# Q and K of pairs 6 to 15 turned in 32x32 blocks by VectorE and regrouped through DRAM, instead of turned by TensorE

## The chip, the core and the metric

One core of a Trainium2 chip runs the whole program. The metric is the device time of one execution in microseconds (us); the time of a kernel is the median of its runs. TensorE (PE) multiplies matrices and writes only to the eight PSUM banks, VectorE (DVE) and ScalarE (ACT) work on elements, GpSimd (POOL) and SyncE (SP) mostly issue transfers (DMAs) here. Each engine works through its own queue in order.

## The reference

Block-sparse attention with batch 4, 8 heads, 768 positions and head size 64, then an MLP mixer on the result:

```python
scores = scale * np.matmul(q, k.transpose(0, 1, 3, 2))
...
scores = np.where(mask, scores, -1000000000.0)
...
attn = attn / (np.sum(attn, axis=-1, keepdims=True) + 1e-09)
return np.matmul(attn, v).astype(np.float32)
...
h = np.maximum(xt @ w_tok1, 0.0) @ w_tok2
u = x + h.transpose(0, 2, 1)
h2 = np.maximum(u @ w_ch1, 0.0) @ w_ch2
return (u + h2).astype(np.float32)
```

The mask lets blocks of 32 positions see their neighbours, the first and the last block, and three drawn blocks each. The scores need Q and K with the head dimension on the partitions, while they are loaded with positions on the partitions, so both must be turned.

## The kernel before, in words

The 32 heads are worked as 16 **pairs** of two heads. For each pair the kernel loads K, Q and V as bf16 (`load_pair`, L458, issued by POOL; token 6p+c goes to partition p), and then:

- **Turn.** `relayout` (L786) copies the raw K or Q into a `lay` tile with the two heads side by side (L811, by VectorE or ScalarE, labels `l` and `L`). `transposes` (L853) turns it on TensorE against an identity matrix, six steps a tensor (label `t`): pairs 1 to 7 as full 128x128 tiles (L910), pairs 8 to 15 as two 64-row tiles at once (L875). A copy out of PSUM puts the result into `ktb` or `qtb`, one of four buffers each (L886 and L923, label `h`; L939 for pairs 1 to 3).
- **Scores.** `scores` (L962, matmul at L974, label `q`): 9 steps a pair, each four matmuls of 256 columns; from pair 4 on the two heads run in the two halves of the array. ScalarE takes the exponential (L984, `e`), VectorE multiplies by the mask (L1001, `x`, two operations for each third of a pair).
- **Values.** V is copied beside a column of ones (L808, `y` and `Y`), multiplied with the exponentials (L1113 with the whole array, L387 with half arrays, `v` and `V`), and VectorE divides (L1069 and L1126 with the line behind each, `n`, one for each third of a pair).
- **Mixer.** Per batch: token mixing (`f`, `g`, `k`, `K`; relus `af`, `ak`; adds `df`, `dk`), a turn of the sum (L1178, L1441, copies `w`), channel mixing (`c`, `C`; relus `r` at L1155 on ScalarE and L1157 on VectorE), and the stores (`o`, L1578 and L1633, issued by SP). The mixer of one batch runs between the attention of the next.

**The order of the work** is written out. `ORDER` (L38) holds a list of labels for each engine, and a planner (`Planner`, L127) walks through the lists with a cost in ns for each step and emits an instruction when its list and its inputs let it. The program that results is fixed: on the chip each engine does its list in that order and waits where an input is late. The costs place an instruction only among those of other engines' queues, such as which DMA issue or fence on SP comes first.

**Half-array chains.** `halves` (L377) sums in two rounds, with lower-case labels for the first and capitals for the second. The two row tiles swap banks in between, and the second round must not start before the first has ended. `fence` (L370, no-op at L373) sees to that: a no-op that waits for the last matmul of the first round, on SP, or on POOL once nearly all loads are through (`pool_free`). The second round's first matmuls wait for the no-op.

```python
late = pool_free.t is not None and pool_free.t < P.now
n = (nc.gpsimd if late else nc.sync).nop()
tc.add_manual_dep(n.ins, mm.ins.name, AFTER, reason=WHY)
```

**A path that is there but not taken.** For pairs from `NPE` on, `relayout` turns the raw tensor in blocks of 32x32 with two VectorE instructions (one a head, 128x384 elements each), and `through_dram` (L829) regroups the blocks: SP puts the tile out to DRAM (192 KB, label `b`) and gets it back in four transfers of 32 partitions (label `u`, runs of 192 elements). `scores` then reads keys with a step of six elements and queries in runs of 32 (L972, L973). Before, `NPE` is 16, so no pair takes it. The planner counts 1050 ns for the two block turns (`TURN`).

Of the kernel before, what the change touches and what calls it, by code (L numbers as in the profile page):

```python
# [28 lines left out]
def spell(text):  # L29

    steps = []
    for word in text.split():
        name = word.rstrip("0123456789")
        steps += [name] * int(word[len(name):] or 1)
    return steps
# [1 line left out]

ORDER = dict(  # L38
    pe=spell("""
        q s3 q s t6 q3 s q v t6 v2 q2 v2 t6 q t v t v t q t3 m q v2 q3 f v f5 v2 f2 q f3 v f q2 v2 q t4 f t  # L40
        f3 t2 f2 t2 v t2 q v f3 q v f3 t q v t4 q f t f2 t v q f9 q v f2 q f q f3 t v t3 v2 q t2 f7 q f3 q
        f2 v q v q v f t2 v f v t4 f q v f5 q t f t f3 t2 f q f v t2 f2 q v f t2 f q t v2 t q f t2 v2 t2 f q
        t f3 t2 f t g12 q f6 t3 g2 t2 g4 t g6 q2 f2 v t g2 t g2 f t2 g2 f3 q t v2 t q c3 q c q2 C4 c11 q C2
        q c C10 q v6 q c3 q c4 C q c C c C c2 C2 c q c3 C c C2 q C7 c C c2 q v9 c q2 C2 k6 C2 K c K c K q K
        c K c K q C4 k4 v4 k2 K4 v2 K2 v3 c v c v c v c3 V7 c2 V2 q V3 C5 q C3 c q c4 q c k c k2 c k2 t3 k
        t3 c2 q c2 k6 q C3 q C3 v9 t3 v t v t2 C2 v q C V12 q C3 q c4 q c3 t6 q c2 v12 q c2 v5 V v4 V v3 V4
        c V17 C V q C3 q C2 t C t5 q C3 t6 C2 q v24 V24 t6 c3 q c k5 q k c2 t K t4 K t K4 c q c2 v11 k v c2
        k2 t V t3 V2 t V t k V8 c K4 C2 k2 q C K2 C2 q C3 k5 t2 k t4 C2 k6 C2 v3 c v2 c v7 c2 t5 V4 t V2 C q
        C2 V C c4 q V5 C3 v C v11 q c2 V12 c6 q2 C8 c2 v12 c2 V4 q V8 C q C3 q c4 q C3 v3 C v9 c4 V q c2 V4
        c2 V2 q V5 C8 c v12 c q c V2 c V10 q C4 q c2 k5 c2 k t q C t C t4 C K C K5 q c8 v5 q v4 C6 v C2 v2  # L50
        k4 V12 q K4 k2 q K2 c3 q c q k6 c4 v9 t v3 t5 c V12 k2 c k4 c2 q v12 C q C V C V11 q C3 q v C4 v4 q
        C2 c2 v7 c2 t2 V9 t V3 t3 c q c3 q c v11 c q v c2 V4 v V4 v3 V C V v5 V2 v3 C2 q V C V4 q V C V2 C
        V4 C2 q C2 k C2 k2 v3 k3 q v5 K v K v2 K v K3 t3 V12 t3 c3 q c k4 q c K4 k2 c3 q K2 c2 q c2 k6 q C4
        q C2 t C t5 q C2 k2 C k4 q C2 v24 V14 q V7 c3 q c V3 q C4 c6 q c C c C t6 C2 c6 v C v2 C v8 C q C v
        c2 C6 V C v C V v2 V v4 V4 v3 V v V4 v13 V15 q V9 c2 q c2 k2 q k3 C2 q k C2 K v K v3 K3 v8 K q V12 q
        k4 c2 q c K3 c K k2 c4 K2 q C8 c4 q v7 C v k6 C v3 C v C k6 v12 V20 c2 q c2 V4 q C4 c2 q c9 q c C c
        v c v C2 v C4 q v4 c v c2 C v4 c2 V3 c V9 q C c C c2 q c6 C c v5 q v7 C6 V2 c v C V4 v V c C2 v V2 v
        C V v4 V v4 V C2 V C V11 C2 c4 k6 c k c k4 c k c6 k4 c k7 c4 k c4 C3 k4 C k5 C2 k3 c182
    """),
    act=spell("""  # L60
        p e37 h e ag e h e9 r e4 r e2 r e5 r l e4 w e3 h e10 h e2 h e l h e2 w e r e8 r e2 r e4 y ak e2 r e4
        h w e5 y e7 ak h e2 l e9 r e r e r2 e4 r e4 r e r e5 r e3 ak r2
    """),
    dve=spell("""
        Z3 z3 Y z H z H z H2 n S H2 Y n H2 m n2 af Y n df H L H n df H2 h L wf Y2 l2 n y af n h df2 n h n l
        wf l h af n l n x h df l df dg2 x wg wf n h x r x3 r n2 l x l x2 y x r x2 n3 l y x r y ak x dk2 n x
        r x h x w x3 n o l x h x2 y n l n x h2 o n2 x l2 x ak x2 l n dk2 l x h w o l h x2 n r n x r x n x r
        x l x n x n r x h r x l x n dk2 x w x n x2 y n x2 o l n h x2 n x n x o y n x2 dk2 x w y x h w o n x
        n x y h x4 n3 x3 ak n x dk2 x2 w2 x n2 r x2 n x3 o n2 dk3 w2 r9 o2 r2 o r4 o2 r o5
    """),  # L70
    sp=spell("""
        s2
    """),
)
AF = mybir.ActivationFunctionType
# [38 lines left out]
TURN = 1050.0  # L114
# [192 lines left out]
def kernel(  # L307
# [14 lines left out]
    B, H, S, D = q.shape  # L322
# [5 lines left out]
    NV = 4  # L328
    NR = 4
    NET = 4  # L330
    NPE = 16
    NT0 = 4

    sb1 = ctx.enter_context(tc.tile_pool(name="sb1", bufs=1))
# [451 lines left out]
    def relayout(p):  # L786
        lays = LAYS[p] = {}
        for nm in ("k", "q", "v") if p >= NT0 else ("v",):
            raw = raws.pop((nm, p))
            arr = arrive.pop((nm, p))  # L790

            def emit(eng, nm=nm, raw=raw):
                copy = nc.scalar.copy if eng == "act" else nc.vector.tensor_copy
                if nm != "v" and p >= NPE:
                    lay = sbw.tile([128, 2, 2, NC * 32], BF16, tag=f"{nm}lay", bufs=2, name=f"{nm}lay{p}")
                    for h in range(2):
                        to = lay[:, h, :, :]
                        if nm == "k":
                            to = to.rearrange("p g (j c) -> p g c j", c=NC)
                        else:  # L800
                            to = to.rearrange("p g (c j) -> p g c j", c=NC)
                        nc.vector.transpose(
                            out=to,
                            in_=raw[:, h, :, :].rearrange("p c (g e) -> p g c e", g=2),
                        )
                    lays[nm] = lay
                elif nm == "v":
                    copy(out=vaug[p % NV][:, :, :, 0:64], in_=raw)  # L808
                else:
                    lay = sbw.tile([128, NC, 2, D], BF16, tag=f"{nm}lay", bufs=2, name=f"{nm}lay{p}")  # L810
                    copy(  # L811
                        out=lay[:, :, :, :], in_=raw.rearrange("p h c d -> p c h d")
                    )
                    lays[nm] = lay

            deps = [arr]
            if nm == "v" and p >= NV:
                deps.append(pv_done[p - NV])
            if nm != "v" and p >= NT0 + 2:
                deps.append(qT_there[p - 2, 1])  # L820
            block = nm != "v" and p >= NPE
            lays[nm + "ev"] = P.op(("dve", "act") if p >= FORM["relay_act"] and not block else ("dve",),
                                  {"dve": TURN if block else 290.0, "act": 660.0}, deps, emit,
                                  label=("y" if nm == "v" else "l") if p >= FORM["relay_act"] else "Y" if nm == "v" else "L")
            copied[nm, p] = lays[nm + "ev"]
        va_there[p] = lays["vev"]
        return lays

    def through_dram(p):  # L829

        lays = LAYS[p]
        for nm, bufs, there in (("k", ktb, kT_there), ("q", qtb, qT_there)):
            where = stage[nm][p % 2]
# [128 lines left out]
    def scores(s, bank, done, rel, exps):  # L962
# [808 lines left out]
```

## Time and profile before

| | |
|---|---|
| median of 3 runs | 249.47 us (249.04 to 249.51) |
| the profiled execution, its own time | 249.75 us |
| its span, first to last instruction | 248.0 us |
| PE busy, share of the span | 241.2 us, 97% |
| VectorE busy | 187.6 us, 76% |
| ScalarE busy | 172.3 us, 69% |
| GpSimd busy | 49.6 us, 20% |
| granted TensorE clock | 0.997 |
| moved by DMA | 21.05 MB, 85 GB/s in the mean |

The profile is one execution. A row of a group reads: source line, engine, operation, output tile, inputs, shapes, count, then busy us and the mean ns of one, then the idle time of the engine just ahead of them and who ended it. PEld is TensorE's weight load, which runs beside the matmul ahead of it. A row of one line (the view by source line) gives shortest, median and longest ns and the first and last start. Rows with an engine name that ends in q (SPq, POOLq) are waits or DMA issues on that engine's queue. Matmuls overlap, so the time that one takes from PE is the distance to the next start and not its mean duration; the trace holds the starts.

Scores of pair 6 start at 64.9 us, those of pair 8 at 90.3, of pair 15 at 183.9; the last end at 198.2. The loads of all pairs are issued by 69.2 us.

### The profile page before, as it was taken

The page shows a single profiled execution, that of the slowest core. Times are in us where ns is not written, and L with a number is a line of the kernel's source. Part 1 is how long each engine was busy: PE and PEld are TensorE (multiplying, and loading weights), DVE is VectorE, ACT ScalarE, POOL GpSimd, SP SyncE. Part 2 cuts the span into 40 slices and gives each one's busy share as a digit, 9 for nine tenths or more (in the row PEclk, how much of TensorE's full clock was granted, in tenths as well). Part 3 has the DMA queues.
Part 4 walks back from the last instruction along what each step waited for, and adds up shares of the span by engine and source line. Part 5 has one row for each costly group of instructions (what it writes and reads, how often), then busy time and mean ns, then how long its engine had stood idle before and what let it go on. Part 6 is the DMA issues. An engine that isn't in the chain of part 4 may idle for free.

```text
span 248.0 us, 9867 instructions
## 1 busy us (share of the span) xinstructions
PE 241.2 (97%) x4446; PEld 175.2 (71%) x4450; DVE 187.6 (76%) x346; ACT 172.3 (69%) x188; POOL 49.6 (20%) x86
## 2 busy tenths in 40 slices
PE   7899989999999999999999999999999999999994
PEld 3689979876777667767778777777887656566442
DVE  5894977989879998999788887986788353388422
ACT  5999989998787988758989978988887610100000
POOL 8948987457510000000000000000000000000000
PEclk9999999999999999999999999999999999999998
DMA  7999999999980022020000022020000010004132
GB/s 172 161 206 207 211 204 203 205 201 201 201 134 3 4 87 90 3 87 3 3 3 3 4 90 83 7 89 3 3 3 5 3 76 11 0 3 157 57 127 85
DMA packets 18969, 21.05 MB, mean 85 GB/s; under 512 B 1328, under 2 KB 16320, under 8 KB 18928
## 3 DMA queue, kind: packets, MB, share of 16 engines
q0 software_dynamic: 15104, 12.98, 33.2%
q1 hardware_dynamic: 3280, 7.06, 7.5%
q8 instruction: 35, 0.57, 0.9%
q10 hardware_dynamic: 544, 0.39, 0.5%
q14 instruction: 6, 0.05, 0.1%
HBM read 26.74 MB, written 6.29 MB: 133 GB/s over the span
## 4 chain that ended last, share of the span: by engine, by line
PE 85%; DMA 5%; POOL 5%; DVE 3%; issue 1%; DVEq 0%; POOLq 0%
PE banks L387 50%; PE banks L974 12%; PE banks L1607 8%; PE banks L1542 6%; DMA kraw<-in_k_dram 5%; PE banks L1113 3%; POOL vraw L458 1%; PE banks L875 1%; PE banks L1382 1%; PE banks L910 1%; POOL kraw L458 1%; POOL qraw L458 1%; PE banks L1178 1%; DVE vaug L808 1%; PE banks L1362 1%
## 5 line engine op out<-in xcount | busy, mean ns | idle before, releaser
L984 ACT ACTIVATE et<-banks 128x1024 bf16<-128x1024 f32 x144 | 139.8, 1026 | 24.4 <-PE banks L974 22.8
L1001 DVE TENSOR_TENSOR et<-et,mask 128x992 bf16<-128x992 bf16 x72 | 65.2, 927 | 3.2 <-ACT et L984 2.9
L974 PE MATMUL banks<-qtb,ktb 64*128 64x256 bf16 (+1 forms) x576 | 62.4, 270 | 1.1 <-DVE x L1127 0.9
L387 PE MATMUL banks<-uT,w_ch 64*128 64x256 bf16 (+1 forms) x576 | 59.7, 322 | 0.0
L387 PE MATMUL banks<-w_ch,rc 64*128 64x512 bf16 x384 | 55.6, 376 | 0.0
L974 PEld LDWEIGHTS <-ktb 64*128 64x128 bf16 (+1 forms) x576 | 32.5, 95 | 14.4 <-issue 1.8
L387 PEld LDWEIGHTS <-et 64*128 64x128 bf16 x1440 | 35.0, 94 | 7.8 <-POOLq L373 0.5
L387 PE MATMUL banks<-vaug,et 64*128 64x65 bf16 x1440 | 40.3, 190 | 0.0
L387 PEld LDWEIGHTS <-w_ch 64*128 64x128 bf16 x576 | 28.0, 94 | 8.9 <-POOLq L373 0.2
L1157 DVE TENSOR_SCALAR rc<-banks 128x512 bf16<-128x512 f32 (+1 forms) x27 | 24.1, 906 | 7.3 <-PE banks L1542 3.9
L1155 ACT ACTIVATE rc<-banks 128x1024 bf16<-128x1024 f32 (+1 forms) x18 | 17.5, 976 | 8.1 <-PE banks L1542 7.4
L387 PEld LDWEIGHTS <-rc 64*128 64x128 bf16 x384 | 18.2, 94 | 6.6 <-issue 0.4
L1607 PE MATMUL banks<-w_ch,rc 128*128 128x512 bf16 (+2 forms) x104 | 21.9, 355 | 0.3 <-issue 0.2
L1113 PE MATMUL banks<-vaug,et 128*128 128x65 bf16 x432 | 18.1, 193 | 0.0
L1113 PEld LDWEIGHTS <-et 128*128 128x128 bf16 x432 | 16.4, 97 | 0.9 <-issue 0.4
L1607 PEld LDWEIGHTS <-rc 128*128 128x128 bf16 x108 | 10.0, 98 | 9.9 <-issue 0.4
L1542 PE MATMUL banks<-uT,w_ch 128*128 128x512 bf16 (+1 forms) x96 | 15.8, 326 | 0.0
L387 PEld LDWEIGHTS <-w_tok 64*128 64x128 bf16 x240 | 12.8, 108 | 3.1 <-DVE a_t L1228 0.2
L1542 PEld LDWEIGHTS <-w_ch 128*128 128x128 bf16 x96 | 9.4, 98 | 6.4
L1070 DVE TENSOR_TENSOR x<-banks,recip 128x256 bf16<-128x256 f32 x30 | 12.7, 424 | 1.0
L1069 DVE RECIPROCAL recip<-banks 128x4 f32<-128x4 f32 x30 | 5.4, 182 | 10.5 <-PE banks L387 9.2
L1621 DVE TENSOR_TENSOR o<-banks,x 128x512 f32<-128x512 f32 x7 | 4.8, 690 | 9.0 <-PE banks L1607 8.0
(124 smaller groups left out, 254.2 us busy)
## 6 DMA issues: line engine op xcount, KB each, us to landing
out_dram<-o SPq DMA_DIRECT2D x8, 512.0 KB, 2.7
w_ch<-in_moe_w_ch_dram POOLq DMA_DIRECT2D x8, 384.0 KB, 9.8
vraw<-in_v_dram POOLq DMA_DIRECT2D x10, 192.0 KB, 7.3
out_dram<-o SPq DMA_DIRECT2D x7, 256.0 KB, 2.0
kraw<-in_k_dram POOLq DMA_DIRECT2D x9, 192.0 KB, 8.5
qraw<-in_q_dram POOLq DMA_DIRECT2D x9, 192.0 KB, 7.5
w_tok<-in_moe_w_tok_dram POOLq DMA_DIRECT2D x2, 384.0 KB, 10.3
qf<-in_v_dram POOLq DMA_DIRECT2D x4, 192.0 KB, 7.5
```

Of the source, the lines that this page charges most:

```text
L387: mms.append(nc.tensor.matmul(out=outs()[o](x), lhsT=lhs(o, x, r), rhs=rhs(o, x, r), start=(back == 0 and x == 0), stop=(back == 1 and x = ...
L458: nc.gpsimd.dma_start(out=raw, in_=APx(src, 2 * p * S * D, [[NC * D, 128], [S * D, 2], [1, NC * D]]),)
L974: nc.tensor.matmul(out=ps[:, hd, 256 * i : 256 * i + 256], lhsT=keys, rhs=rhs, start=(i == 0), stop=(i == 1),)
L984: nc.scalar.activation(out=ets[p, t][:, jj, :, :, :].rearrange("k i h q -> k h i q"), in_=ps.rearrange("k h (i q) -> k h i q", i=2), func= ...
L1001: nc.vector.tensor_tensor(out=et, in0=et, in1=free(mask[:, 2 * lo, 256 * t + EDGE : 256 * t + EDGE + 1], 0, [[S, 2 * n], [0, 2], [1, w]]), ...
L1069: nc.vector.reciprocal(out=recip[:, :, :], in_=free(po, 64, [[512, 2], [65, 2]]))
L1070: nc.vector.tensor_tensor(out=free(xs[b][:, pb // 2, 2 * t, 128 * (pb % 2) : 128 * (pb % 2) + 128], 0, [[64, 2], [256, 2], [1, 64]],), in0 ...
L1113: nc.tensor.matmul(out=po[:, hd, c, :], lhsT=et[:, jj, i, hd, 128 * c : 128 * c + 128], rhs=va[:, hd, 2 * jj + i, 0:65], start=(jj == 0 an ...
L1155: nc.scalar.activation(out=o(), in_=src(), func=AF.Relu)
L1157: nc.vector.tensor_scalar(out=o(), in0=src(), scalar1=0.0, scalar2=None, op0=ALU.max)
L1542: nc.tensor.matmul(out=in_bank(pbox["pm"], [k, 128 * n])[:, x // 4, :], lhsT=w_ch1[:, x % 4, 128 * cc : 128 * cc + 128], rhs=st[b]["uT"][: ...
L1607: nc.tensor.matmul(out=pbox["pm"][:, 0:n], lhsT=box["rc"][:, cc, 128 * sc : 128 * sc + 128], rhs=w_ch2[:, cc, lo : lo + n], start=(cc == 0 ...
```

## The change

`NPE` goes from 16 to 6, so Q and K of pairs 6 to 15 take the path through VectorE and DRAM. Their 20 block turns have a label of their own (`T`, VectorE only). All four orders are written anew: TensorE's list has 60 `t` in place of 180, VectorE's 20 `T`, and SP's 20 `b` and 20 `u`. ScalarE's list loses 8 `h` and 3 `l` and gains 4 `r`, 2 `y`, 1 `af` and 1 `ak`; VectorE's loses 12 `h`, 17 `l` and those eight. The rest of TensorE's steps are the same in number and stand in another order.

```diff
 ORDER = dict(
     pe=spell("""
-        q s3 q s t6 q3 s q v t6 v2 q2 v2 t6 q t v t v t q t3 m q v2 q3 f v f5 v2 f2 q f3 v f q2 v2 q t4 f t
...
+        s q s3 q2 v s q2 v2 q t9 q t3 v q v2 t2 q v t4 q2 v2 q2 t v t3 f2 t2 f v f4 q v f4 q f m q2 t4 q t
...
     dve=spell("""
-        Z3 z3 Y z H z H z H2 n S H2 Y n H2 m n2 af Y n df H L H n df H2 h L wf Y2 l2 n y af n h df2 n h n l
-        wf l h af n l n x h df l df dg2 x wg wf n h x r x3 r n2 l x l x2 y x r x2 n3 l y x r y ak x dk2 n x
...
+        Z3 Y z6 n H2 S H2 n H2 Y n H2 n m af df Y n H2 L df H n wf H h l af L n2 Y df l h y df n h wf Y T n
+        T n h n x T df2 dg2 x wg wf n x2 T x2 y n2 x2 y r x2 T r x2 n3 x r x ak x T dk2 x n T w x T x n o x2
+        y x2 n x2 n o n2 x2 T2 x n x dk2 T2 o x n x2 r T x n x r n x T x3 n T r n x y r x T n dk2 x2 w2 x2 n
+        x n x o x3 n y n T n x2 o x n T x dk x dk T w x w o n2 x2 r T x4 n3 x2 ak x n x2 dk2 w n y w r x3 r
+        n x4 n o n2 dk3 w2 r5 o r7 o2 r o7
     """),
     sp=spell("""
-        s2
+        s2 b2 u2 b2 u b u b u2 b2 u2 b2 u2 b2 u b u b3 u2 b u3 b2 u b u2
     """),
 )
...
-    NPE = 16
+    NPE = 6
...
             lays[nm + "ev"] = P.op(("dve", "act") if p >= FORM["relay_act"] and not block else ("dve",),
-                                  {"dve": TURN if block else 290.0, "act": 660.0}, deps, emit,
-                                  label=("y" if nm == "v" else "l") if p >= FORM["relay_act"] else "Y" if nm == "v" else "L")
+                                  {"dve": TURN} if block else {"dve": 290.0, "act": 660.0}, deps, emit,
+                                  label="T" if block else ("y" if nm == "v" else "l") if p >= FORM["relay_act"] else "Y" if nm == "v" else "L")
```

More of the change, by code (lines that the diff above doesn't have):

```diff
@@ L39 @@
     pe=spell("""
-        q s3 q s t6 q3 s q v t6 v2 q2 v2 t6 q t v t v t q t3 m q v2 q3 f v f5 v2 f2 q f3 v f q2 v2 q t4 f t
[L41 to L58, printed above, removed]
+        s q s3 q2 v s q2 v2 q t9 q t3 v q v2 t2 q v t4 q2 v2 q2 t v t3 f2 t2 f v f4 q v f4 q f m q2 t4 q t
@@ new lines @@
+        f7 t f v3 f q t2 f3 t4 q v2 q t v t2 q f6 t3 q f8 q f v f q2 f v f q v q v3 q f5 t f t2 v t3 v f q
+        f2 t f t2 f t f q t3 v t q t f3 t f3 q t q2 v3 f v f3 v q f v f4 q f v t f v2 f q2 f5 g f g3 f2 g f2
+        g7 f2 q2 g12 f3 q f2 q2 g6 f v3 c q c3 q c3 C q c C7 c2 q c3 v6 q c5 q c2 C3 q C5 q C4 c5 q c C c2 q
+        c C2 c3 q C6 c C c2 C q C c v9 q C2 q C c C c k2 c k4 c q K5 q K C4 c3 k5 c3 K3 k K v c2 v8 K2 v C
+        v2 C4 V C3 c V c V2 c V3 q c2 q V5 c4 q c2 k c k5 q C2 q C v5 C2 v2 k v5 k5 C V5 C q V6 C2 V C q C2
@@ new lines @@
+        c q c4 q c q c2 v c2 v11 q c V2 c V v2 V4 v5 V2 C v V3 C v2 q v2 C2 V C V C q V C2 V3 v V2 C V4 C3 q
+        v23 V24 q c2 q c3 k3 q k3 c2 v K v8 K v3 K q K V6 K V K V2 c4 V3 c q k4 C q K4 C k2 C2 K2 q C3 v4 C
+        v3 k6 v C2 v k6 v3 C2 V c4 V2 q V3 C4 V6 c2 q c2 q c2 C4 c3 q c3 v12 C4 q C c V2 C c C2 V c2 V9 q C4
+        q v12 c2 V12 c2 q2 C c C c7 C7 v4 q v3 C v5 C2 c V3 c2 V c V8 q C2 q C2 c2 v12 c2 V12 q C2 q C k6 q
+        C K4 c3 K2 c4 q c v12 k4 V12 K2 q K2 C4 k2 C4 K2 c2 q c3 q k c k3 c k c q k c3 k c k5 q C v12 C q V3
@@ new lines @@
+        C V6 C V v2 V v V v4 C v2 C q v3 C2 V6 q V6 C2 q C2 c2 q c4 q c v7 c q v c v4 c2 V v V v5 V v V c v2
+        V3 v V v3 V3 v V C V v2 V3 v3 V v V2 v V3 v V2 v C q v C2 V10 q V C V C q C3 q C k5 C k C q K3 v12
+        K3 V12 q c5 q k4 c q K c K3 c q c2 k2 c2 K2 q C4 q k C k3 C k2 C q C2 v C v9 k4 v k2 v C2 V6 v3 V4
+        v8 V2 v c2 V2 c V2 c V8 q C c2 C q C c2 q C5 c5 q c5 C q C c C4 v3 C2 c v8 q v C3 V7 v C v2 V5 v19
+        V12 v2 q c V12 c q c2 q k2 C2 k3 q k C2 K6 v12 q V12 q c8 q k2 C k2 C q K3 C K C2 k2 C3 K2 c4 v9 q C
@@ L59 @@
+        k4 v3 k C k C2 V12 c q c3 k q k5 C4 q c13 q2 C2 c3 C5 q C c4 v12 C q C v C v V v V11 v2 C3 v C v q
+        v3 c C v2 c3 C V v2 c v V2 C v V C V2 c V c v c V3 v V2 v2 c v3 c v c2 v V v2 V3 C v C V v C V v5 V
+        v C v C V11 C V6 C c5 k12 c8 k2 c k6 c k3 c k c C6 k12 c187
     """),
     act=spell("""
-        p e37 h e ag e h e9 r e4 r e2 r e5 r l e4 w e3 h e10 h e2 h e l h e2 w e r e8 r e2 r e4 y ak e2 r e4
-        h w e5 y e7 ak h e2 l e9 r e r e r2 e4 r e4 r e r e5 r e3 ak r2
+        p e37 af e2 ag e8 r2 e5 r e3 r e5 r2 e5 w e6 y e6 y e ak e3 w2 e r e4 r e4 r e r e5 ak e2 r e11 y2
@@ L63 @@
+        e5 ak e10 r e2 r e r e4 r e4 r e r e8 ak r5
     """),
     dve=spell("""
-        Z3 z3 Y z H z H z H2 n S H2 Y n H2 m n2 af Y n df H L H n df H2 h L wf Y2 l2 n y af n h df2 n h n l
-        wf l h af n l n x h df l df dg2 x wg wf n h x r x3 r n2 l x l x2 y x r x2 n3 l y x r y ak x dk2 n x
-        r x h x w x3 n o l x h x2 y n l n x h2 o n2 x l2 x ak x2 l n dk2 l x h w o l h x2 n r n x r x n x r
-        x l x n x n r x h r x l x n dk2 x w x n x2 y n x2 o l n h x2 n x n x o y n x2 dk2 x w y x h w o n x
@@ L69 @@
-        n x y h x4 n3 x3 ak n x dk2 x2 w2 x n2 r x2 n x3 o n2 dk3 w2 r9 o2 r2 o r4 o2 r o5
+        Z3 Y z6 n H2 S H2 n H2 Y n H2 n m af df Y n H2 L df H n wf H h l af L n2 Y df l h y df n h wf Y T n
+        T n h n x T df2 dg2 x wg wf n x2 T x2 y n2 x2 y r x2 T r x2 n3 x r x ak x T dk2 x n T w x T x n o x2
+        y x2 n x2 n o n2 x2 T2 x n x dk2 T2 o x n x2 r T x n x r n x T x3 n T r n x y r x T n dk2 x2 w2 x2 n
+        x n x o x3 n y n T n x2 o x n T x dk x dk T w x w o n2 x2 r T x4 n3 x2 ak x n x2 dk2 w n y w r x3 r
```

## The prediction

> **What bounds the kernel now.** I read the forty slices of the page first, then the busy time by stretch, then the groups by line, and last the fences of the half-array chains. The slices (share busy in tenths, each slice 6.2 us):
>
> ```profile
> PE   7899989999999999999999999999999999999994
> DVE  5894977989879998999788887986788353388422
> DMA  7999999999980022020000022020000010004132
> ```
>
> TensorE is full nearly from the start to the end, VectorE is at nine tenths only from slice 11 to 19, and DMA is full until about 74 us and nearly empty behind. By stretch (columns: engine time, its instructions in brackets, then clock, DMA share, GB/s):
>
> ```profile
> 33.00:124.00 91.00, 91.00 (x1935) 69.05 (x1935) 79.33 (x140) 78.10 (x85) 23.01 (x33) 1.00 0.61 106
> ...
> 124.00:203.00 79.00, 79.00 (x1834) 59.18 (x1828) 61.55 (x100) 64.11 (x69) 0.00 (x0) 1.00 0.06 23
> ```
>
> PE is busy for 91.00 of 91.00 us and 79.00 of 79.00. Its ends are modelled, so I checked starts: from 33 to 203 us, starts come later than the columns of the matmul ahead explain by 2.0 us in all, most of it pauses of 0.09 us where PE goes from full tiles to 64-row tiles or back. So between 33 and 203 us **TensorE is the path**: a nanosecond taken off it is gained, and a nanosecond of waiting is lost. VectorE idles 91.0 - 79.3 = 11.7 us in the first stretch and 17.4 in the second. Its densest part with PE still full is this one, 27.97 of 30 us, 93.2%:
>
> ```profile
> 80.00:110.00 30.00, 30.00 (x757) 21.30 (x754) 27.97 (x49) 23.88 (x27) 0.00 (x0) 1.00 0.15 55
> ```
>
> **TensorE: removed.** Four groups by line (count, busy us, mean ns):
>
> ```profile
> L875 PE MATMUL banks<-ident,klay 64*128 64x64 bf16 x96 | 3.8, 190 | 0.0
> L910 PE MATMUL banks<-ident,qlay 128*128 128x128 bf16 x24 | 3.7, 220 | 0.0
> L875 PE MATMUL banks<-ident,qlay 64*128 64x64 bf16 x96 | 3.5, 189 | 0.0
> ...
> L910 PE MATMUL banks<-ident,klay 128*128 128x128 bf16 x24 | 3.2, 219 | 0.2 <-DVE x L1127 0.2
> ```
>
> A mean of 190 ns is latency; the price is the distance between starts. Half-array turns run two at once and such pairs start 29 ns apart, full ones 56. Pairs 8 to 15 lose 96 such starts (2.8 us), pairs 6 and 7 24 full ones (half of L910's 48: 1.3 us): 4.1 us, and about two changes of tile size around 42 to 50 us, 0.2. **Term: -4.3 us.**
>
> **TensorE: added.** The keys of pairs 6 to 15 become weights with a step of 6 elements. The second token weights have that step already, and load slower than the first:
>
> ```profile
> L1382 PEld LDWEIGHTS <-w_tok 128*128 128x128 bf16 x48 | 3.9, 126 | 0.5 <-issue 0.4
> ...
> L1362 PEld LDWEIGHTS <-w_tok 128*128 128x128 bf16 x48 | 3.4, 97 | 0.1
> ```
>
> Behind a step of 109 ns or more, starts show no cost (109 either way); behind a 29 ns value step, the strided step in the half-array form took 122 to 127 ns, so +15. The new order has 20 of 90 score steps behind such a step: +0.3 us (ends 0 and 90 x 15 = 1.4). The moving queries now come in runs of 32 elements; the nearest rows are runs of 128, at full rate; I take nothing. Each pair's scores then wait for eight landings instead of two copies, and further waits are instructions of their own on PE's queue: three such rows in before took 51 ns each, two of them without a mark on the starts. 10 pairs x 5 x 51 ns = 2.6 us at most, 0 at least; I take **+0.6**, from one in three showing in full, less what the matmuls ahead cover.
>
> **VectorE.** Removed by the order strings and rows: 12 copies out of PSUM (0.557 us each), 17 regroupings (0.352 quiet); moved to ScalarE: 4 relus, 2 value copies, 2 small ones. Added: 20 "T", each two block turns of 128x384 bf16. No row shows a turn. Lower end: two copies of 0.35, 0.70 us, since no copy of this tensor is faster. Upper end: two operations of 0.69, the row of 512 elements out of PSUM, 1.38. I take the row with the same 384 elements, the nearest in size, since no row says that a turn runs at the packed rate of a plain copy: 2 x 0.553 = 1.11 us (the plan in the code allows 1.05):
>
> ```profile
> L1391 DVE TENSOR_TENSOR x<-banks,x x8: 547/553/558, 23.4 to 47.0; 128x384 bf16<-128x384 f32 x8
> ```
>
> The Trainium skill ("VectorE: DVE Perf Modes", The three transpose paths) speaks against it: it gives 311 ns for one 128x128 bf16 turn on VectorE, and in blocks of 32x32 only. By that figure, an estimate would be 6 x 0.311 = 1.87 us a T, 0.76 more than mine, 11 us over fifteen of them; no run here shows it yet.
>
> Fifteen T lie between the 8th and 30th normalisation, which run at 33 and 124 us now. There VectorE loses 8 x 0.557 + 14 x 0.352 + 2 relus of 1.23 + 1.7 small ones = 13.5 us and gains 15 x 1.11 + 0.7 = 17.4: net +3.9. PE gets shorter there by 1.3 + 60 x 29 ns = 3.1. The first two T stand where the copies at 38.6 and 39.6 us took 0.55 and 0.60 instead of 0.35 while POOL issues loads: 2 x 1.11 x 0.6 = +1.3. Idle time left: 11.7 - 3.9 - 3.1 - 1.3 = 3.4 of 87.9 us, 96% busy. At the densest that is shown with PE full (6.8% idle) it needs 6.0. PE waits for the rest, exponentials masked late and banks freed late: **+2.6** (0 if T is 0.94 or less; 15 x 0.27 = 4.1 more at 1.38). ScalarE stays about level there (-8 copies, +8 of the moved ones).
>
> **DMA and the queues.** Each of 20 tensors goes out in one transfer of 192 KB and back in four, with runs of 384 bytes. Order places them a pair or more ahead of use (T of pair 8 behind the 15th and 18th normalisations, at 58 and 68 us now; its scores start at 90), so against 2.0 us from issue to landing of a 256 KB store, or 7.5 (median) of a load in the crowd, landing is hidden; uncovered it would cost some 5 us a pair. "DMA: Bandwidth & Descriptors" of the skill (Specifications) wants runs of 512 bytes or more for full rate; no row here has 384-byte runs on this queue, and with landing hidden the term is the same by either.
>
> What is not hidden is what stands behind them **on SP**. The second half of a half-array chain waits for a fence, a no-op on SP until the loads are nearly through, then on POOL:
>
> ```profile
> L373 POOLq EVENT_SEMAPHORE  x71: 17/17/17, 73.2 to 202.0; - x71
> L373 SPq EVENT_SEMAPHORE  x9: 17/17/17, 51.0 to 71.5; - x9
> ```
>
> Nine fences go by SP in 20.5 us, and PE waits for them 0.3 us now. By the order, two gets (pair 7) and three puts fall there. An issue of 128 rows took SP 0.42 to 0.46 us early on (0.33 quiet, 0.83 for 24 rows): 2 x 4 x 0.45 + 3 x 0.45 = 4.95 us, 24% of the time. Nine fences x 24% x half a get (0.9) = 2.0; the order leaves room between halves, so I take a third off: **+1.4** (ends 0, and 9 x 44% x 1.65 = 6.5 with 0.83 an issue). A get that waits for its own put holds the queue longer. On POOL the fences start behind the last load: four tensors out and back, 1.6 MB at the 200 GB/s that the loads fill, delay it by up to 8 us; loads have over 20 us in hand, but a fence at 72 us may wait: +0.3 (0 to 3).
>
> **Sum:** -4.3 + 0.3 + 0.6 + 2.6 + 1.4 + 0.3 = +0.9 us on the profiled execution's 249.75 (span 248.0 and 1.75 around it): 250.65. The median of the runs is 0.28 lower, so **250.4**.
>
> **Rivals.**
> *VectorE keeps up (ends faster).* A T of 0.94 us or less, or a plan that puts turns into gaps that forced idle time leaves, makes the 2.6 zero: -1.7, 247.8 (246.9 to 248.9). For it: VectorE has 17 us to spare behind 124 us. Against: only five T are there. It decides at 0.94 us a T.
> *The whole gain.* Fences and waits cost nothing as well: -4.3 + 0.3, 245.5, up to 246.9. For it: PE waits for fences 1.2 us in all today.
> *It cancels.* Half the shortage (1.3) and fences at 1.4: 249.1, up to 249.9.
> *A turn is dear, or gets stand waiting.* T at 1.38: 250.4 + 4.1 = 254.5; or three gets of pairs 7 and 8 each hold SP for 2 us: 254 to 256 with a fence behind each. That turns leave TensorE cannot fail: the order has 60 steps in place of 180.
>
> **Chances.** Forecast (250.0 to 252) 0.33, dear 0.13, cancels 0.12, VectorE keeps up 0.27, whole gain 0.15. A measurement tells 0.2%, 0.5 us, from no change. Faster 0.42, same 0.12, slower 0.46. The range leaves out the lower half of the whole gain and the upper part of the dear case: 246.0 to 254.4; the forecast's own is 250.0 to 252.
>
> **What would show it.** Right: PE still "full" but with gaps of over 0.1 us ahead of L974 or L387, released by DVE or ACT, between 40 and 124 us; DVE at 95% or more there; a T of two rows near 0.55 us; fence waits on SP grown from 0.3 to over 1 us. Wrong: a turn row far from 0.55 either way; PE starts as dense as now; score steps longer than 109 ns everywhere (strided operands dear, up to 90 x 2 x 15 ns and more); or loads so late that first use of a pair waits for DMA.

## The result, and the profile after

Before 249.49 us (249.04 to 249.82, 4 runs), after **259.75 us** (258.60 to 260.61, 4 runs): ratio 1.041, 95% interval 1.0365 to 1.0454. The profiled execution of after took 259.53 us, its span is 257.8 us, and the granted clock is 0.991. The forecast was 250.4 and the range ended at 254.4: slower, as its largest chance said, but 5.35 us beyond the end of the range. Runs of a kernel that took over 1.5% longer than its fastest are slow runs, and the medians and ranges given here leave them out.

The slices of after, in the order of those shown of before, with the clock between:

```profile
PE   7989997995999899899889998999999999999994
...
DVE  6867888994998999999999899999886773249422
...
PEclk9999999799999999999999999999999999999998
DMA  7999999999999352234211221523200002002332
```

PE is no longer full: there are holes at slices 7 and 10 (39 to 45 and 58 to 64 us), the clock drops between them, and 8s stand among the 9s up to slice 25. VectorE is at eight tenths or, mostly, nine from slice 11 to 30. By stretch (columns as before: engine time and instructions, then clock, DMA share, GB/s):

```profile
33.00:64.00 31.00, 26.27 (x421) 20.32 (x421) 25.77 (x49) 24.16 (x28) 17.99 (x28) 0.94 1.23 213
...
80.00:110.00 30.00, 28.30 (x649) 21.69 (x645) 28.15 (x42) 23.39 (x25) 0.00 (x0) 1.00 0.39 109
110.00:124.00 14.00, 12.79 (x270) 9.99 (x267) 13.93 (x19) 11.27 (x12) 0.00 (x0) 1.00 0.40 119
```

Before, PE was busy for every microsecond of these. Now it lacks 4.7 us in the first stretch, where VectorE has 5 us to spare, and 2.9 us in the other two, where VectorE is busy for 42.08 of 44 us. These are two different losses. PE's waits from 30 to 210 us name them, longest first:

```profile
PE banks L387 <- SPq L373: 2.9, 1, 2.9
PE banks L974 <- DVE x L1070: 1.9, 2, 1.1
PE banks L1113 <- DVE x L1127: 1.5, 1, 1.5
PE banks L974 <- DVE rc L1157: 0.9, 1, 0.9
...
```

One wait for a fence on SP, and a row of waits for VectorE (the third belongs to the early part, loss three).

**Loss one, VectorE.** The rows of the turns by source line (shortest, median, longest ns, first and last start):

```profile
L802 DVE STREAM_TRANSPOSE klay<-kraw x8: 1461/1522/1595, 67.3 to 120.5; 128x384 bf16<-128x384 bf16 x8
L802 DVE STREAM_TRANSPOSE qlay<-qraw x8: 533/553/676, 78.8 to 127.4; 128x384 bf16<-128x384 bf16 x8
```

The same operation on the same shape: Q's takes 0.553 us, the very row that the forecast took, and K's 1.522, 2.75 times as long. Q is written in runs of 32 elements (`"(c j)"` in the code of the turn), K with a step of six elements, 12 bytes (`"(j c)"`). A pair's two halves take 1.11 us for Q and 3.04 for K by rows; K's two overlap a little, so VectorE is held for 2.78:

```profile
103.23 2.78 DVE L802 STREAM_TRANSPOSE klay<-kraw 128x384 bf16<-128x384 bf16 x2
105.72 1.13 DVE L802 STREAM_TRANSPOSE qlay<-qraw 128x384 bf16<-128x384 bf16 x2
106.77 0.64 DVE L1001 TENSOR_TENSOR et<-et,mask 128x992 bf16<-128x992 bf16 x1
107.32 0.18 DVE L1069 RECIPROCAL recip<-banks 128x4 f32<-128x4 f32 x1
107.53 0.42 DVE L1070 TENSOR_TENSOR x<-banks,recip 128x256 bf16<-128x256 f32 x1
```

And on PE, in the same execution:

```profile
106.76 0.40 PE L387 MATMUL banks<-w_ch,rc 64*128 64x512 bf16 x2
108.01 0.42 PE L974 MATMUL banks<-qtb,ktb 64*128 64x256 bf16 x4 [0.85 <-DVE x L1070]
```

A division that frees a PSUM bank stands behind both turns and a mask in VectorE's queue, and the next score step waits for that bank. That is one of seven such pauses of 0.7 to 1.2 us between 86 and 171 us.

**Loss two, SP.** SP's queue from 53 to 64 us, and PE at the end of it (start, length, what):

```profile
53.92 0.35 SPq L836 DMA_DIRECT2D kstage<-klay  x1
55.45 0.34 SPq L836 DMA_DIRECT2D qstage<-qlay  x1
61.31 1.75 SPq L843 DMA_DIRECT2D ktb<-kstage  x4
```

```profile
63.17 0.50 PE L387 MATMUL banks<-uT,w_ch 64*128 64x256 bf16 x6 [2.87 <-SPq L373]
```

SP puts K of pair 7 out at 53.92. The get of the same tensor stands next but one in the queue and waits 5.5 us for the put to land. The DMA engines are full of loads here (share 1.23 to 1.29 until 80 us): this put took 7.3 us, the longest; later, in the quiet, a put took 1.9. Then come four issues, 1.75 us, and only then the fence that a half-array chain waits for. PE stands for 3.0 us.

**Loss three, the early part.** PE pauses 1.66 us at 41.0 us and 0.5 at 44.1, and the clock falls to half behind them, from 44.8 to 48.2 us:

```profile
40.00:44.00 4.00, 2.51 (x54) 1.96 (x53) 3.91 (x8) 2.43 (x4) 2.84 (x5) 1.00 1.30 203
44.00:49.00 5.00, 4.66 (x52) 3.72 (x47) 4.96 (x9) 3.40 (x5) 2.02 (x3) 0.66 1.19 231
```

In these 3.4 us the steps of 56 ns take 107. The pause comes from VectorE, whose first turn waits 1.5 us for its load, with the divisions behind it. Going back along the waits: GpSimd issues the loads, and ahead of them it waits 6.0 us for the block mask, which VectorE now copies at 21.1 us (17.6 before), because the new order has the step `m`, which makes the mask, later:

```profile
POOL mask L760 <- DVE maskb L746: 6.0, 1, 6.0
```

The experiments take the three apart.

### The profile page after: what moved, and what is told of

Its sections match the earlier page's. It is cut to its first block, busy times and chain, and to the rows that moved or that the text cites. A ratio compares the mean times of both kernels' runs of the same rounds, so it can differ in the third digit from the quotient of the medians.

```text
span 257.8 us, 9612 instructions
## 1 busy us (share of the span) xinstructions
PE 240.6 (93%) x4234; PEld 179.3 (70%) x4234; DVE 204.3 (79%) x349; ACT 170.4 (66%) x185; POOL 49.7 (19%) x86
## 2 busy tenths in 40 slices
DMA packets 33370, 28.91 MB, mean 112 GB/s; under 512 B 13169, under 2 KB 30721, under 8 KB 33329
## 4 chain that ended last, share of the span: by engine, by line
PE 58%; DVE 17%; DMA 12%; POOL 6%; issue 4%; ACT 1%; SPq 1%; DVEq 0%; POOLq 0%
PE banks L387 33%; DVE klay L802 8%; PE banks L1607 8%; PE banks L974 6%; PE banks L1542 6%; DMA w_tok<-in_moe_w_tok_dram 4%; DMA klay_first<-in_k_dram 3%; DVE et L1001 3%; DMA kstage<-klay 3%; DMA ktb<-kstage 2%; POOL mask L760 2%; DVE x L1070 1%; DVE rc L1157 1%; POOL vraw L458 1%; PE banks L1113 1%
## 5 line engine op out<-in xcount | busy, mean ns | idle before, releaser
L387 PE MATMUL banks<-uT,w_ch 64*128 64x512 bf16 (+1 forms) x576 | 60.8, 322 | 3.4 <-SPq L373 2.9
L387 PE MATMUL banks<-w_ch,rc 64*128 64x512 bf16 x384 | 57.8, 376 | 0.0
L974 PEld LDWEIGHTS <-ktb 64*128 64x128 bf16 (+1 forms) x576 | 39.4, 114 | 13.6 <-issue 4.4
L387 PEld LDWEIGHTS <-et 64*128 64x128 bf16 x1440 | 38.1, 94 | 11.2 <-issue 2.0
L387 PE MATMUL banks<-vaug,et 64*128 64x65 bf16 x1440 | 43.7, 190 | 1.5 <-DVE uT L1189 0.8
L387 PEld LDWEIGHTS <-w_ch 64*128 64x128 bf16 x576 | 29.8, 94 | 12.1 <-SPq L373 3.4
L1157 DVE TENSOR_SCALAR rc<-banks 128x512 bf16<-128x512 f32 (+1 forms) x23 | 21.2, 931 | 11.2 <-PE banks L1542 6.9
L1155 ACT ACTIVATE rc<-banks 128x1024 bf16<-128x1024 f32 (+1 forms) x22 | 20.3, 927 | 12.4 <-PE banks L1542 8.6
L387 PEld LDWEIGHTS <-rc 64*128 64x128 bf16 x384 | 21.0, 94 | 5.4 <-issue 0.3
L1113 PE MATMUL banks<-vaug,et 128*128 128x65 bf16 x432 | 17.6, 193 | 2.0 <-DVE x L1127 1.5
L802 DVE STREAM_TRANSPOSE klay<-kraw 128x384 bf16<-128x384 bf16 x8 | 11.1, 1525 | 0.0
```

The costliest lines, as they stand in the source:

```text
L387: mms.append(nc.tensor.matmul(out=outs()[o](x), lhsT=lhs(o, x, r), rhs=rhs(o, x, r), start=(back == 0 and x == 0), stop=(back == 1 and x = ...
L802: nc.vector.transpose(out=to, in_=raw[:, h, :, :].rearrange("p c (g e) -> p g c e", g=2),)
L974: nc.tensor.matmul(out=ps[:, hd, 256 * i : 256 * i + 256], lhsT=keys, rhs=rhs, start=(i == 0), stop=(i == 1),)
L1113: nc.tensor.matmul(out=po[:, hd, c, :], lhsT=et[:, jj, i, hd, 128 * c : 128 * c + 128], rhs=va[:, hd, 2 * jj + i, 0:65], start=(jj == 0 an ...
L1155: nc.scalar.activation(out=o(), in_=src(), func=AF.Relu)
L1157: nc.vector.tensor_scalar(out=o(), in0=src(), scalar1=0.0, scalar2=None, op0=ALU.max)
```

## The experiments

Some of them read keys in the wrong order, which is said at each. Ratios are to runs of before taken along with the kernel (medians 249.2 to 249.4 us). The table counts, from the starts of the matmuls, what PE lost: each distance to the next start beyond the steady one for that number of columns (29 ns for 65, 56 for 128, 109 for 256), if more than 25 ns over. "Work" is the span less all that is lost. The time is the median of the runs, all else is of the profiled execution.

| kernel | us | DVE busy | work | lost to 40 us | 40 to 80 | 80 to 200 | lost in all |
|---|---|---|---|---|---|---|---|
| before | 249.49 | 187.6 | 238.9 | 6.0 | 1.5 | 0.5 | 9.1 |
| after | 259.75 | 204.3 | 236.3 | 5.4 | 9.0 | 6.7 | 21.5 |
| k_dense_write | 252.31 | 189.1 | 236.1 | 4.8 | 9.3 | 0.2 | 14.6 |
| late_gets | 257.27 | 204.6 | 235.9 | 5.2 | 7.8 | 6.7 | 21.0 |
| k_dense_late_gets | 249.12 | 189.4 | 235.3 | 5.1 | 5.2 | 0.8 | 12.2 |
| late_mask_first | 255.12 | 203.7 | 235.5 | 4.9 | 5.0 | 6.8 | 17.9 |
| dense_late_mask_first | 246.66 | 189.2 | 235.2 | 4.7 | 3.0 | 0.6 | 9.5 |

**K written densely.** K is turned as Q is; the scores still read with a step of six, so pairs 6 to 15 meet keys in the wrong order. All else is after.

```diff
-                        if nm == "k":
-                            to = to.rearrange("p g (j c) -> p g c j", c=NC)
-                        else:
-                            to = to.rearrange("p g (c j) -> p g c j", c=NC)
+                        to = to.rearrange("p g (c j) -> p g c j", c=NC)
```

> The changed kernel with one edit: the block turn of K writes its 32x32 blocks one behind the other, as Q's does, instead of with a step of six elements. The scores still read keys with the step, so they meet the wrong keys (the size of all work is the same; the result of pairs 6 to 15 is not the reference's). Theory 'dear turn' (a K turn row is 1.52 us against 0.55 for Q, and VectorE's 19 us more make PE wait): K rows fall to about 0.55 us, VectorE loses about 19 us, and the time falls by at least 7 us, to 249 to 252.5. Rival 'queues' (fences behind gets on SP, landings, and DMA in the crowd hold PE, and VectorE only follows): rows fall as well, but the time stays above 256.

252.31 us (250.82 to 254.57), ratio 1.0126 (1.0056 to 1.0196). The loss from 80 to 200 us falls from 6.7 to 0.2 and PE is busy for all 44.00 us from 80 to 124; the loss before 80 us stays. The stretch in question:

```profile
80.00:124.00 44.00, 44.00 (x985) 31.55 (x982) 40.24 (x67) 36.70 (x40) 0.00 (x0) 1.00 0.39 114
```

So the dear turn is the larger cause, 7.4 us, and not the only one. The run also clears the strided keys, the queries in runs of 32 and the longer waits of PE: all are still there, and PE is full.

**Q written with the step too**: the reverse, one line the other way (queries of pairs 6 to 15 in the wrong order).

> The changed kernel with Q's block turn written with a step of six elements as well (scores read Q as before, so they meet wrong queries). Theory 'dear turn': Q rows rise from 0.55 to about 1.52 us, VectorE gets another 19 us, and with VectorE already the limit most of it shows: 270 to 279 us. Rival 'queues': VectorE's rows rise but the time stays below 264.

271.01 us in a single run. Q's rows take K's time:

```profile
L799 DVE STREAM_TRANSPOSE qlay<-qraw 128x384 bf16<-128x384 bf16 x8 | 11.2, 1539 | 0.0
```

So it is the step, not the tensor, its buffer or its place. VectorE's busy time goes 189.1, 204.3, 220.2 over the three kernels and the time 252.3, 259.75, 271.0: the first 15 us cost 7.4, the next 16 cost 11.3. That less slack is left would explain it, but it is not shown: the clock also stood at half for 10.2 us in this run, against 3.4 in after.

**A price list of steps.** In one kernel, K of pairs 6, 7, 14 with step 1, of 8 and 9 with step 2, of 10 and 11 with step 3, of 12, 13, 15 with step 6 (keys in the wrong order in most).

```diff
+                        elif p in (8, 9):
+                            nc.vector.transpose(
+                                out=to.rearrange("p g (x j y) -> p g x y j", x=3, y=2),
+                                in_=src.rearrange("p g (x y) e -> p g x y e", y=2),
+                            )
```

> The changed kernel as a price list: K of pairs 6, 7 and 14 is written with step 1, of 8 and 9 with step 2, of 10 and 11 with step 3, of 12, 13 and 15 with step 6 as in the change (scores meet wrong keys for all but the last three). If the price goes by how many elements share 16 bytes of a row (8, 4, 2 or 3, 1 or 2), rows read about 0.55, 0.55 to 0.8, 0.8 to 1.1 and 1.52 us; if any step other than 1 is dear, 0.55, then 1.52 three times. By 'dear turn' the time lies between 250 and 257, by 'queues' above 256.

The groups by line, of step 6, 2, 1 and 3 in this order (busy us, mean ns):

```profile
L814 DVE STREAM_TRANSPOSE klay<-kraw 128x384 bf16<-128x384 bf16 x2 | 2.8, 1529 | 0.0
...
L804 DVE STREAM_TRANSPOSE klay<-kraw 128x384 bf16<-128x384 bf16 x4 | 2.1, 583 | 0.0
L802 DVE STREAM_TRANSPOSE klay<-klay_first 128x384 bf16<-128x384 bf16 x4 | 2.1, 554 | 2.0 <-DMA klay_first<-in_k_dram 2.0
...
L809 DVE STREAM_TRANSPOSE klay<-kraw 128x384 bf16<-128x384 bf16 x2 | 1.5, 816 | 0.0
```

0.55, 0.58, 0.82, 1.53 us: two elements apart cost 5%, three 47%, six 176%, as the first of the two expectations had it. The kernel took 255.42 us in a single run, between the dense and the strided one.

**Gets placed later**, with K dense, and in the exact kernel. `CLASH` is what the planner adds to a put's landing while loads run; with more of it, the gets are placed behind more fences.

```diff
-CLASH = 2000.0
+CLASH = 4500.0
```

> K's turn written densely as before, and a put counted 2.5 us longer while loads run (CLASH 4500 for 2000), so that a get is queued later on SP, behind fences that it stood ahead of. Scores of pairs 6 to 15 meet wrong keys, as in the run with the dense turn. Theory 'fence behind a get': of the 5 us or so by which that run lost PE time between 33 and 64 us, 3 to 4 us are the one fence that stood behind a get whose put had not landed; it goes, and the time is 247 to 249.5. Rival 'crowd': landings are slow for everyone, the wait turns up elsewhere, and the time stays at 251 or more.

> The changed kernel with that one constant (CLASH 4500): K's turn stays dear. Exact result. Theory: the fence wait of 3 us near 60 us goes and the rest stays: 256 to 257.5. Rival: with VectorE the limit, the wait was covered by its backlog and the time stays at 259 to 260.

With K dense 249.12 us (247.38 to 250.36), ratio 0.9993 (0.9969 to 1.0017); exact 257.27 (255.96 to 258.66), 1.0307 (1.0271 to 1.0343). That is 3.2 and 2.5 us less than without it, and PE's longest wait for SP in the exact kernel falls from 2.9 us to this:

```profile
PE banks L387 <- SPq L373: 0.5, 1, 0.5
```

So the get that stands waiting is a cause by itself and adds to the dear turn. The whole of its 3.0 us does not come back in the exact kernel: in the profiled execution the early pause is 3.0 us long instead of 1.66, and the clock stays at half for 6.8 us instead of 3.4.

**The early mask.** First TensorE's step `m` alone goes from the 69th to the 42nd place (the expectation says 49th), in both kernels with late gets:

```diff
-        ... q2 v2 q2 t v t3 f2 t2 f v f4 q v f4 q f m q2 t4 q t
+        ... q2 m v2 q2 t v t3 f2 t2 f v f4 q v f4 q f q2 t4 q t
```

> The kernel with the dense K layout and the late gets (keys of pairs 6 to 15 wrong, 249.12 us), and TensorE's mask step m put back from its 69th to its 49th place, near its 47th of before. Theory (the new order's early part is a third cause): the mask is ready at 18 us again and not at 21, GpSimd's loads go out some 2 to 3 us earlier, the first block turn no longer waits for its load, the clock does not fall near 45 us: -1.0 to -2.0, 247.1 to 248.1. Rival (the loads are bound by the DMA engines, not by GpSimd's issues, and the early loss of clock comes from elsewhere): 248.8 to 249.5, the first block turn waits as before.

> The exact kernel with late gets (257.27 us) and the mask step put back in the same way. Theory: the same 1 to 2 us, 255.3 to 256.3, and the pause of TensorE near 41 us (3.0 us in the trace of the late gets) goes. Rival: 257 again.

249.16 us (248.18 to 249.70), ratio 0.9982 (0.9967 to 0.9998), and 256.83 (256.06 to 257.65), 1.0294 (1.026 to 1.0329): next to nothing. But the traces show that this did not test the theory: the copy started at 21.2 and 20.6 us, since `m` on VectorE stands behind two copies and a normalisation of its own list. So that was moved as well:

```diff
-        Z3 Y z6 n H2 S H2 n H2 Y n H2 n m af df Y n H2 ...
+        Z3 Y z6 n H2 S H2 n H2 Y n m H2 n af df Y n H2 ...
```

> The exact kernel with late gets and the earlier mask step on TensorE (256.83 us), with VectorE's mask copy (m) now put ahead of the two copies (H) and the normalisation that stand in front of it, as it stood in before. Moving TensorE's step alone moved the mask only from 21.1 to 20.6 us. Theory (the late mask holds GpSimd's loads and with them the first block turns): the mask copy starts by 18.5 us, the wait of the first block turn for its load falls from 2.1 us to under 0.7, the pause of TensorE near 42 us (1.8 us) to under 0.7: 255.0 to 256.0. Rival (the first turn of a K costs 3 us in front of the masks that TensorE waits for, whenever its load comes): the pause stays, 256.3 to 257.2.

> Dense K layout (keys of pairs 6 to 15 in the wrong order), late gets, early mask: all three suspected causes taken away at once. Theory (the three are all there is, and what is left is the removal of turns from TensorE): 246.5 to 248.5, faster than before by 0.4 to 1.2%; TensorE pauses no longer than 10 us in all. Rival (with K dense the early mask brings nothing, because VectorE has the time to wait): 248.8 to 249.4.

Exact: 255.12 us (254.87 to 255.36), ratio 1.0236 (1.022 to 1.0251). The copy starts at 17.2 us, GpSimd's wait for it is this:

```profile
POOL mask L760 <- DVE maskb L746: 1.3, 1, 1.3
```

The first turn waits 0.4 us for its load instead of 2.1, and the clock stays at 1.00 between 40 and 53 us. -1.7 us, as the theory said; the pause near 42 us is down to 0.6, but one of 1.2 us at 46.2 is there, behind an addition on VectorE.

K dense as well, so that all three causes are gone: **246.66 us** (245.86 to 247.90), ratio **0.9892** (0.9856 to 0.9928), faster than before. Its slices and the two stretches in question:

```profile
PE   7999999999999999999999999999999999999993
...
DVE  6876889999877899999988989898778753179322
```

```profile
80.00:110.00 30.00, 30.00 (x694) 21.87 (x692) 27.79 (x47) 25.59 (x29) 0.00 (x0) 1.00 0.45 139
110.00:124.00 14.00, 14.00 (x320) 10.38 (x316) 12.81 (x23) 11.77 (x13) 0.00 (x0) 1.00 0.19 59
```

PE is full again with VectorE at 92% in both, and loses 9.5 us in all, much as before. What is left is the shorter work, 235.2 against 238.9 us. So the three causes together account for the loss.

The early mask does not act at the same place in both kernels. With K dense and late gets, no pause of TensorE from 40 to 70 us is longer than 0.5 us to begin with; there the late loads hold the first fence on GpSimd, which stands behind the last load (issued at 75.3 us). With the early mask that load goes out at 72.8. PE's longest wait for a fence on GpSimd, without the early mask and with it:

```profile
PE banks L387 <- POOLq L373: 1.8, 1, 1.8
...
PE banks L387 <- POOLq L373: 0.4, 1, 0.4
```

**Exact kernels with cheap turns.** Four tries to get the dense price and the keys in order. *Step 2* in the turn and the rest of the order by the transfers, in runs of 128 bytes, with late gets; and the same for pairs 10 to 15 alone, in the order of before, where loads are over.

```diff
+                if nm == "k":
+                    for b in range(4):
+                        nc.sync.dma_start(
+                            out=APx(where, 64 * b, [[4 * S, 32], [256, 12], [1, 64]]),
```

> An exact version without the dear turn: K is written with a step of two elements (0.58 us in the price list), put out in four transfers with runs of 64 elements, and got back in four with whole rows, so that keys are read with a step of two; and gets queued later as above. It should do as the dense turn with late gets does, within 1 us, if transfers of 128-byte runs are hidden too: 247 to 250. If short runs or three more puts on SP matter, 251 or more.

> The kernel before, with only pairs 10 to 15 through VectorE and DRAM, K with step two as above, in the order of before: nothing of it falls into the time of the loads, and all fences are on POOL by then. Exact result. PE loses 72 x 29 ns = 2.1 us; VectorE gains 12 x 1.1 and loses 10 x 0.35 and 7 x 0.56, +5.8 us, from 85 us on, where it idles 20 us. If the crowd and the fences on SP were what was left beside the dear turn: 247 to 248.5. If the path itself costs (waits for landings on PE, VectorE near full from 80 to 124 us): 249.5 or more.

261.70 us (259.82 to 263.58, two runs), ratio 1.0502 (1.041 to 1.0595), in the expectation's range for transfers that are not hidden (251 or more): four puts a tensor instead of one, 23888 packets under 512 bytes instead of 13169, and PE waits 7.7 us for two fences and 2.4 for landings. From pair 10 on 252.66 us (252.37 to 252.79), 1.0138 (1.0117 to 1.0158), in the range given for a path that costs by itself: the last fence on SP is through by 72 us, before any get, but VectorE is busy for 42.36 of the 44 us from 80 to 124, in an order that was not made for it; PE lost 1.57 us in one wait at 99.7.

*The strided write on another engine*: VectorE turns densely, GpSimd or ScalarE copies with the step of six before the put.

```diff
+                if nm == "k":
+                    six = lays["kraw"].rearrange("p h c d -> p (h c d)").rearrange("p (x j c) -> p x j c", x=4, c=NC)
+                    nc.gpsimd.tensor_copy(        # nc.scalar.copy
+                        out=six.rearrange("p x j c -> p x c j"),
+                        in_=lays[nm][:, :, :, :].rearrange("p h g (c j) -> p (h g) c j", c=NC),
+                    )
```

> The same kernel made exact: VectorE turns K into the dense layout (1.1 us), and GpSimd, which does little behind 75 us, copies it into the layout with a step of 6 before it goes out. Theory (VectorE's 2 us more for each K were the cost; GpSimd has room): 247.5 to 250. Rival (GpSimd's copy of 768 elements with a step of 6 is slow, holds its loads ahead of 70 us and the fences behind, or slows VectorE): 252 to 258.

> The same with ScalarE in place of GpSimd for the copy. Theory (a copy of this size took ScalarE some 0.7 us, ten of them 7 us on an engine that is 69% busy): 248.5 to 251.5. Rival (a step of 6 elements makes ScalarE's copy as dear as VectorE's turn, or the copy waits in ScalarE's queue for its turn and holds exponentials): 252 to 257.

272.77 us (272.51 to 274.12), ratio 1.0945 (1.0911 to 1.0979), and 270.48 (268.87 to 271.33), 1.0854 (1.0812 to 1.0896): the rivals, and further out. Rows of the copies, GpSimd's and ScalarE's kernel:

```profile
L836 POOL COPY kraw<-klay 128x768 bf16<-128x768 bf16 x4 | 13.0, 3247 | 37.1 <-DVE klay L799 20.0 <-PE banks L1187 17.1
```

```profile
L836 ACT COPY kraw<-klay 128x768 bf16<-128x768 bf16 x4 | 11.0, 2758 | 0.0
```

A plain copy of the same 768 elements takes ScalarE 0.84 us (V, in the same trace); with the step 2.76, 3.3 times as long. So ScalarE pays for the step as VectorE does. GpSimd's ten copies took 2.75 to 3.74 us; no run has its dense copy of this size. ScalarE's copies delay exponentials (PE waits for them 8.1 us), and GpSimd's first stands among its loads, so that a put, a get and the fence behind them come 19 us late:

```profile
PE banks L387 <- SPq L373: 20.2, 2, 19.3
```

*Q alone*, which is cheap to turn as it is, in the order of before, with K left to TensorE: from pair 6 on, the same with late gets, and from pair 10 on with late gets.

```diff
-                if nm != "v" and p >= NPE:
+                if nm in 'q' and p >= NPE:
```

> The kernel before with Q alone of pairs 6 to 15 through VectorE and DRAM, K on TensorE as before, in the order of before with Q's turn steps and their copies taken out. Exact result. PE loses 12 x 56 + 48 x 29 ns = 2.1 us, VectorE gains ten turns of 1.11 us and loses eight regroupings of 0.35 and six copies of 0.56, +4.9 us. Theory 'dear turn' (a Q turn is not dear): 247.5 to 249.5. Rival 'queues': fences behind ten gets cost more than the 2.1 us, 250.5 or more.

> The kernel in which only Q of pairs 6 to 15 goes through VectorE and DRAM, in the order of before (254.53 us), with CLASH at 4500 so that gets are placed later. Every block turn here is a cheap one of 1.1 us. Theory (a fence behind a get that waits for its put cost this kernel 2.7 us near 54 us): 251.5 to 252.3, the wait of TensorE for SP there under 0.5 us. Rival (the 5 us that it lies above before are the order's own: turns of VectorE between copies and masks, not the queue): 254 to 255.

> Q alone of pairs 10 to 15 through VectorE and DRAM, CLASH at 4500, the rest as before (Q alone from pair 6 on: 250.65). Theory (a cheap turn of 1.11 us takes the place of a regrouping of 0.35 and a copy out of PSUM of 0.56 on VectorE or ScalarE, so that VectorE loses little and TensorE gains 36 starts of 29 ns, 1.0 us, where no load and no fence on SP is in the way): 248.3 to 249.2, faster than before by 0.1 to 0.5%. Rival (the order was not made for it, so the gain is lost in new waits of TensorE for VectorE): 249.5 to 250.7.

254.53 us (253.12 to 254.90), ratio 1.0196 (1.0164 to 1.0228); 250.65 (250.21 to 251.79), 1.0054 (1.0035 to 1.0073); 250.37 (249.91 to 250.59), 1.0034 (1.0017 to 1.0052). The first goes to its rival 'queues' (250.5 or more). Late gets give 3.9 us here: the pause of 2.65 us for a fence at 53.9 us is gone. That confirms the second cause in a third kernel, with more than its theory gave. The last line missed its forecast (248.3 to 249.2): PE's work gets only 0.7 us shorter than before and new waits ahead of scores, 0.53 us at 102.5 for VectorE and 0.65 at 145.2 for an exponential of ScalarE, take it back; waits like these were its rival. No exact kernel that was run beats before.

## Why the prediction was wrong, point by point

Between the kernel with everything cured and after lie 259.75 - 246.66 = 13.1 us. On the way through the exact kernels: late gets 2.5, the earlier mask 0.4 + 1.7, and dense K (255.12 to 246.66) 8.5. Against these stand 2.7 us that the change gives when nothing is in its way. 13.1 - 2.7 = 10.4, against a loss of 10.3 that was measured. The shares hold for this order of cures: K dense gives 7.4 as the first of them and 8.5 as the last.

- **TensorE removed, -4.3, and strided weights, +0.3: right, somewhat large.** PE's work fell from 238.9 to 235.2 us with K dense, 3.7, and to 236.3 in after. Weight loads of the scores grew from 95 to 114 ns in the mean and stayed hidden.
- **PE waits for eight landings, +0.6: next to nothing.** In after 32 waits of 51 ns stand there instead of 3. The kernels with K dense and the same gets are full from 80 to 124 us, and the one wait for a landing that the last of them shows is 0.2 us.
- **VectorE, +2.6: the step that failed.** "I take the row with the same 384 elements" gave 1.11 us for every T. It holds to the last digit for Q. For K the write has a step of six elements, which the code of the turn says (the text above the prediction tells of the step only where the scores read the keys), and I priced both by one row with a dense output. A T of K takes 3.04 us by rows and holds VectorE for 2.78. My upper end, 1.38, was a row with a dense output as well, so the range could not hold this. The measured cost is 7.4 us with the other causes in place, 8.5 without. By the same working, with 2.78 for K, some eight K turns between the 8th and 30th normalisation add 8 x 1.67 = 13.4 us where 3.4 were idle: the term would have been 2.6 + 13.4 = 16.0, so the method would have shown the loss and put it too high.
- The other side: at 1.11 us for every T, VectorE costs nothing (0.6 us lost from 80 to 200 us, 0.5 before). *VectorE keeps up* was the better case at that price, though it asked for 0.94. The 96% busy from 33 to 124 us does not come either: in the kernel with everything cured it is 81.93 of 91 us, 90%. Part of that is the +1.3 for turns that run while GpSimd issues loads: in after the first Q pair of turns, at 42.6 us, took 1.03 us.
- **The skill's figure.** 311 ns for 128x128 made 1.87 us a T; Q's row is 0.553 us for 128x384, 0.18 per 128 columns. The estimate from it erred high for the dense write (1.11) and low for the strided one (3.04). Another page would have warned: the Trainium skill ("SBUF — State Buffer", Door 1: The DMA port swizzle) tells of lines of 16 bytes and a penalty for each access to a new line, needing two hits per line for full rate. At 12 bytes a step there are, by an estimate from these figures, 1.33 hits a line, and the write was 2.75 times as long. But the page also lets bf16 stride 8 elements for free, and it would pass a step of 3, with 2.67 hits; here 3 cost 47% and 6 cost 176%. The measurement decides.
- **SP fences, +1.4: right place, half the size, wrong form.** I spread shares of issue time over nine fences. It was one fence behind one get that waited 5.5 us for its own put, 2.5 to 3.9 us by three kernels. I had the mechanism ("a get that waits for its own put holds the queue longer") and put it among the rivals.
- **POOL, +0.3: right in after**, where no fence on GpSimd held PE's weight loads for more than 0.2 us. With K dense and late gets one near 73 us held PE for 1.8, within the 0 to 3. And GpSimd was where the third cause ran through.
- **The order: not priced.** I counted which labels the lists gain and lose, and took a step that is only moved as free. One of those, `m`, made the mask copy start 3.5 us later, and GpSimd's load of K of pair 6 go out at 30.6 us instead of 28.9: 1.7 us exact, 2.5 with K dense.
- **Landing hidden: right** for later pairs; the first two tensors pay through loss two.

*A turn is dear, or gets stand waiting* (254 to 256, 0.13) named both larger causes, but as alternatives. They came together, with a third.

## What to carry to other kernels

Price an instruction by a row with the same access pattern on both sides, output too; a row with the same shape alone was off by 2.75 times here. A wait in an in-order queue of transfers is paid by the fence behind it, so place a get by when its put lands in the crowd, not in the quiet. When an order is written anew, follow what each early step releases on other engines, above all the queue that issues loads.

## What the hardware showed that I had not expected

- A VectorE block turn of 128x384 bf16: 0.55, 0.58, 0.82, 1.53 us with output steps of 1, 2, 3, 6 elements. ScalarE's copy of 768 elements goes from 0.84 to 2.76 us with the step of 6, and GpSimd's with that step takes 2.75 to 3.74.
- The clock fell to half for 3.4 us behind pauses of 1.66 and 0.5 us within 4 us, but not behind one of 3.03 us at 59.9 (1.00 from 58 to 80 us). With late gets and only TensorE's `m` moved it fell, at 43.6 us, at the end of one of 1.82 us. A pause's length alone does not decide it here. The Trainium skill ("TensorE: Matmul & The Clock Gate", Why this matters for your kernels) asks for no gap over some 3 us; here the clock fell behind shorter ones and did not fall behind one of 3.03.
- A put of 192 KB landed after 1.9 us behind 100 us and after 5.2 to 7.3 us with the loads running.
- PE can be full with VectorE at 92%; the first 15 us more on VectorE cost 7.4 us, the next 16 cost 11.3 (a single run, with the clock at half for longer).
